# Gated linear attention and a two-layer feed-forward block in one kernel: the first weight matrix in its own row order, attention in half chunks of 64 tokens

## The chip, the cores and the metric

The kernel runs on one core of one Trainium2 chip. The metric is device time in microseconds for one execution of the whole program. The core has a matrix engine (TensorE, PE in the profile, with its weight loads as PEld), a vector engine (VectorE, DVE), a scalar engine (ScalarE, ACT), GpSimd (POOL), and SyncE (SP), which here issues every DMA transfer. Each engine takes its own instructions in order; engines wait for each other through semaphores. Matmul results go to PSUM, which the kernel splits into eight banks.

## The reference

Four batches, eight heads, 768 tokens, head size 48. The recurrence keeps a 48×48 state for each batch and head:

```python
for t in range(S):
    state = alpha[:, :, t, :, None] * state + einsum('bhd,bhe->bhde', k[:, :, t], v[:, :, t])
    y[:, :, t] = einsum('bhd,bhde->bhe', q[:, :, t], state)
x = y.transpose(0, 2, 1, 3).reshape(3072, 384)
h = x @ w_in                       # 384 x 2048, arrives as float64
g = h * clip(h + 3, 0, 6) / 6
out = g @ w_out                    # 2048 x 384, arrives as float64
```

## The kernel before

**Tiling.** Tokens are cut into 24 chunks of C = 128, six to a batch. Heads are handled in pairs (NP = 4): a pair fills 128 partitions, each head padded from 48 to 64. For a chunk the cumulated decay R and its inverse P come from two scans on VectorE (`decay`, `growth`); keys are multiplied by R and queries by P (`scaled`), so that within a chunk the recurrence is a masked matrix product, and across chunks a product with one state. Two chunks form a group of 256 tokens for the feed-forward part.

**Attention steps of a chunk.** `scores` forms keys × queries: below chunk 8 in eight full 128×128 products, from chunk 8 (SWAP) in halves, leaving out the quarter that the mask would erase. `masked` multiplies the result by the triangle into A on VectorE. `within` multiplies A by v in blocks of 32 output rows; from chunk 8 it needs a copy of half of v (`keep_v`, into v0, on ScalarE). `across` adds the product of the state with the queries, 12 matmuls of 128 columns, in every chunk but the first of a batch. `keep_x` copies the sum out of PSUM as x. For the state, keys are needed with tokens on partitions: below chunk 8 by transposes on TensorE (`k_by_token`, `keep_k`), from chunk 8 through memory outside the core (`turn_k` in 32×32 blocks on VectorE, `write_k` in one transfer, `read_k` in four). `update` multiplies them by v into a 128-partition block whose useful parts are two 48×48 corners a pair; `next_state` adds these to the decayed state on VectorE in two instructions of 48 partitions, and `decayed_state` multiplies by the next chunk's decay on GpSimd. The last chunk of a batch needs no update.

**Feed-forward.** Groups 0 and 1 use plain products (`ff1`, `ff2`). From group 2 the first layer is computed in 20 products of quarter size with sums before and after (M on TensorE, `combine_x` and `output1` on VectorE, `keep1` on ScalarE, the gate `gate1`/`hidden1` on ScalarE and VectorE), and from group 1 the second in 7 products (P on TensorE, `combine_g` and `output2` on VectorE). The float64 weights arrive as pairs of 32-bit words in 16 slices (`load_weight`) and are turned into float32 by bit operations on ScalarE, VectorE and GpSimd (steps d1, d2, dx, d3, d4).

**What sets the order.** One long list of words, written out by hand or by a tool, gives the order of all steps: a word such as `sc.9.1.2` is step, chunk and PSUM banks. Each engine gets its share of the list in that order. The first layer's rows are loaded in the order `(p t r)`, 32 partitions at a time, because `within` and `across` put pair p at partitions 32p of x:

```python
return ps_t["y", j][32 * p : 32 * p + 32, kk]        # L516, y_of
```

Four of the eight PSUM banks serve attention (`bank_t`), four the feed-forward part. The words `z` are matmuls on the identity that only keep TensorE busy at the start. Lines: scores L383, L385 (from chunk 8) and L408; masks L391 and L416; v copies L399; transposes to tokens L428; key turns L453 and L455; key write L459 and read L466; decay L471; update L488 and L494; state sums L507 and L509; within L529, L533 and L539; across L549; first layer L693, its copies L699; second layer L796; weight transfers L184 and L187.

Of the kernel before, what the change touches and what calls it, by code (L numbers as in the profile page):

```python
# [17 lines left out]
def kernel(  # L18
# [43 lines left out]
    GT = G * C  # L62
    W = C + 1
# [3 lines left out]
    HB = C // 2  # L67
# [10 lines left out]

    tri = consts.tile([C, 3, HB], mybir.dt.bfloat16, tag="tri")
    nc.gpsimd.memset(tri, 1.0)  # L80
    for n, b in ((0, 0), (0, 1), (2, 0), (1, 1)):
        at = slice(HB * b, HB * b + HB)
        nc.gpsimd.tensor_copy(out=tri[at, n], in_=mask[at, at])

    v0 = consts.tile([C, H, 64], FP, tag="vfirst", name="vfirst")
    nc.gpsimd.memset(v0, 0.0)
# [9 lines left out]
    for r in range(max(NR, NV)):  # L96
        for name, pad, n in (("a", 1.0, NR), ("k", 0.0, NR), ("q", 0.0, NR), ("v", 0.0, NV)):
            if r >= n:
                continue
            if name == "v":  # L100
                t = consts.tile([C, H, 64], FP, tag=f"v{r}", name=f"v{r}")
            else:
                t = rings[:, 3 * r + "akq".index(name)]
            eng = nc.vector if r == 0 else nc.gpsimd
            if name == "v":
                t4 = t.rearrange("s (p a) e -> s p a e", a=2)
                eng.memset(t4[:, :, 0, D:64], pad)
                eng.memset(t4[:, :, 1, 0 : 64 - D], pad)
            else:
                eng.memset(t[:, :, D:64], pad)  # L110
            ring[name, r] = t
# [16 lines left out]
    st, sm = [], []  # L128
    for r in range(2):
        t = consts.tile([C, NP, 2 * D], FP, tag=f"st{r}")  # L130
        nc.gpsimd.memset(t, 0.0)
        st.append(t)
    for r in range(2):
        t = consts.tile([C, NP, 2 * D], FP, tag=f"sm{r}")
        nc.gpsimd.memset(t, 0.0)
        sm.append(t)
# [35 lines left out]
    def load_weight(i):  # L172
        u = 2 if wide else 1
        dst = weight_dst(i)
        m = dst.shape[1]
        to = raw_of(i).rearrange("p (m n) w -> p m (n w)", m=m) if wide else dst
        if i < NW1:
            n = NSL // KT
            src = moe_w_in[:, u * i * n : u * (i + 1) * n].rearrange(
                "(p t r) f -> p r t f", p=NP, t=KT)  # L180

            for p in range(NP):
                queue = nc.sync
                queue.dma_start(out=to[32 * p : 32 * p + 32], in_=src[p])  # L184
        else:
            o = (i - NW1) * m * C
            nc.sync.dma_start(  # L187
                out=to, in_=moe_w_out[o : o + m * C, :].rearrange("(f p) n -> p f n", p=C))
# [45 lines left out]
    def add_low(i):  # L234
# [9 lines left out]
    bank_t = [ps.tile([C, NP, C], FP, tag=f"t{i}", name=f"t{i}_ps") for i in range(4)]  # L244
    Rs, Qs, Ks, kbs, As = (
        [consts.tile([C, *shape], FP, tag=f"{name}{r}", name=f"{name}{r}") for r in range(2)]
        for name, shape in (("R", (NP * W,)), ("q", (NP, C)), ("k", (NP, C)), ("kb", (NP, C)),
                            ("A", (H, C))))
    Ps = consts.tile([C, NP * W], FP, tag="P", name="P")

    def bank(name, j, i):
        ps_t[name, j] = bank_t[i]
        return ps_t[name, j]
# [35 lines left out]
    def load_v(j, z):  # L289
        v_t[j] = ring["v", z]  # L290
        to = v_t[j].rearrange("s (p a) e -> s p a e", a=2)
        sv = rows(v, j).rearrange("(p a) s d -> s p a d", a=2)
        if j >= SWAP:
            for b in range(2):
                for g in range(2):
                    at = slice(HB * (b ^ g), HB * (b ^ g) + HB)
                    for a in range(2):
                        e = (64 - D) * a
                        nc.sync.dma_start(
                            out=to[HB * b : HB * b + HB, 2 * g : 2 * g + 2, a, e : e + D],  # L300
                            in_=sv[at, 2 * g : 2 * g + 2, a])
            return
        nc.sync.dma_start(out=to[:, :, 0, 0:D], in_=sv[:, :, 0])
        nc.sync.dma_start(out=to[:, :, 1, 64 - D : 64], in_=sv[:, :, 1])
# [65 lines left out]
    SWAP = 8  # L370

    def score_blocks(t):
        return t.rearrange("s p r -> s (p r)")[:, 0 : 2 * 3 * HB].rearrange(
            "s (x n t) -> s x n t", x=2, n=3)

    def scores_of_halves(j, *at):
        sc = [bank("sc%d" % o, j, at[o]) for o in range(2)]
        for h in range(H):
            p, a = divmod(h, 2)
            r, g = slice(64 * a, 64 * a + D), p // 2  # L380
            to = score_blocks(sc[a])[:, p % 2]
            k, q = K_t[j][r, p], Q_t[j][r, p]
            nc.tensor.matmul(to[HB * g : HB * g + HB, 0 : 2 + g : 1 + g], k[:, 0:HB],  # L383
                             q.rearrange("r (n t) -> r n t", n=2), start=True, stop=True)
            nc.tensor.matmul(to[HB * (1 - g) : HB * (2 - g), 1 + g], k[:, HB:C], q[:, HB:C],  # L385
                             start=True, stop=True)

    def masked_halves(j):
        A_t[j] = As[j % 2]
        for o in range(2):  # L390
            nc.vector.tensor_tensor(  # L391
                out=score_blocks(A_t[j][:, NP * o : NP * (o + 1)]),
                in0=score_blocks(ps_t.pop(("sc%d" % o, j))),
                in1=tri.unsqueeze(1).to_broadcast([C, 2, 3, HB]), op=ALU.mult)

    def keep_v(j):
        for b in range(2):
            at, h = slice(HB * b, HB * b + HB), slice(NP * b, NP * b + NP)
            nc.scalar.copy(out=v0[at, h], in_=v_t[j][at, h])  # L399

    def scores(j, *at):
        if j >= SWAP:
            return scores_of_halves(j, *at)

        sc = [bank("sc%d" % o, j, at[o]) for o in range(2)]
        for h in range(H):
            r = slice(64 * (h % 2), 64 * (h % 2) + D)
            nc.tensor.matmul(sc[h % 2][:, h // 2], K_t[j][r, h // 2], Q_t[j][r, h // 2],  # L408
                             start=True, stop=True)

    def masked(j):
        if j >= SWAP:
            return masked_halves(j)
        A_t[j] = As[j % 2]
        for o in range(2):
            nc.vector.tensor_tensor(  # L416
                out=A_t[j][:, NP * o : NP * (o + 1)], in0=ps_t.pop(("sc%d" % o, j)),
                in1=mask.unsqueeze(1).to_broadcast([C, NP, C]), op=ALU.mult)
# [4 lines left out]
    def k_by_token(j, i=None):  # L423
        if not last(j):
            t = bank("kb", j, i)
            for p in range(NP):
                if j < SWAP or p < 2:
                    nc.tensor.transpose(t[:, p], K_t[j][:, p], ident)  # L428
                    continue
                for b in range(2):  # L430
                    nc.tensor.transpose(t[HB * b : HB * b + HB, p],
                                        K_t[j][:, p, HB * (1 - b) : HB * (2 - b)], ident)
# [579 lines left out]
```

## Time and profile before

| | |
|---|---|
| median of three runs | 547.78 us (547.0 to 548.17) |
| the profiled execution's own time | 547.54 us |
| its span, first to last instruction | 545.8 us |
| TensorE busy | 537.1 us, 98% of the span |
| VectorE busy | 476.9 us, 87% |
| ScalarE busy | 202.9 us, 37% |
| GpSimd busy | 51.9 us, 10% |
| DMA queue q1 | 98448 packets, 51.87 MB, 38.9% of 16 engines |

The page gives the busy time of each engine, the chain of work that ended last (followed back from the last instruction to whatever released each step), groups of instructions by line, and the transfers. In the lists of groups a line reads: line, engine, operation, output and inputs with shapes, count, then busy time and mean duration, then the engine's idle time ahead of them. Durations of consecutive instructions overlap, so the distance between two starts is the cost in a full stretch.

### The profile page before, as it was taken

To read this page: it belongs to the slowest core of one execution; us is meant where nothing else is said; L and a number is where in the kernel's file an instruction comes from. 1 tells how busy PE (TensorE), PEld (TensorE's weight loads), DVE (VectorE), ACT (ScalarE), POOL (GpSimd) and SP (SyncE) were. 2 spreads that over 40 slices of the span, in tenths; PEclk is the share of its full clock that TensorE was granted. 3 is DMA by queue.
4 is the path that set the end of the run, shared out by engine and by line. 5 is a ranking of instruction groups with operands and counts; after the bars stand their busy time and mean duration, and the time that the engine had idled before them with its cause. 6 is when DMAs were issued, how large, how long until landed. Compare 5 with 4: busy or idle time off the path is not lost.

```text
span 545.8 us, 14868 instructions
## 1 busy us (share of the span) xinstructions
PE 537.1 (98%) x6222; PEld 511.3 (94%) x6222; DVE 476.9 (87%) x822; ACT 202.9 (37%) x358; POOL 51.9 (10%) x76
## 2 busy tenths in 40 slices
PE   8999999999999999999999999999999999999997
PEld 8888977789899999999999999999999999999996
DVE  7989989999999999999999999999899796465471
ACT  2666664003443342353233233333334332342330
POOL 3333334200000000000000000000000200000000
PEclk9999999999999999999999999999999999999999
DMA  9996677140433552343535342335353110000001
GB/s 182 210 222 127 203 228 186 41 121 17 89 88 81 151 154 49 85 121 89 136 83 154 98 100 49 84 89 157 73 132 95 44 23 16 8 3 23 23 0 37
DMA packets 98515, 52.82 MB, mean 97 GB/s; under 512 B 51472, under 2 KB 91664, under 8 KB 98448
## 3 DMA queue, kind: packets, MB, share of 16 engines
q1 hardware_dynamic: 98448, 51.87, 38.9%
q8 instruction: 49, 0.80, 0.6%
q14 instruction: 18, 0.15, 0.1%
HBM read 43.71 MB, written 8.13 MB: 95 GB/s over the span
## 4 chain that ended last, share of the span: by engine, by line
PE 78%; DVE 12%; DMA 5%; SPq 3%; issue 1%; ACT 0%; POOL 0%; DVEq 0%; POOLq 0%
PE m_ps L796 32%; PE m_ps L693 30%; PE m_ps L571 3%; DMA raw<-in_moe_w_in_dram 2%; PE t_ps L549 2%; PE t_ps L383 2%; PE t_ps L529 1%; PE m_ps L625 1%; SPq L284 1%; PE t_ps L533 1%; DMA g_sb<-in_moe_w_in_dram 1%; DVE g_sb L740 1%; PE t_ps L314 1%; DVE rings L740 1%; PE t_ps L488 1%
## 5 line engine op out<-in xcount | busy, mean ns | idle before, releaser
L699 ACT COPY g_sb<-m_ps 128x512 f32<-128x512 f32 x110 | 63.8, 585 | 158.9 <-PE m_ps L693 130.5
L796 PE MATMUL m_ps<-w,g_sb 128*128 128x192 f32 x704 | 121.7, 326 | 0.0
L796 PEld LDWEIGHTS m_ps<-w,g_sb 128*128 128x128 f32 x704 | 113.8, 190 | 0.6 <-issue 0.2
L796 PE MATMUL m_ps<-rings,g_sb 128*128 128x192 f32 x528 | 91.3, 326 | 0.7 <-DVE rings L740 0.7
L796 PEld LDWEIGHTS m_ps<-rings,g_sb 128*128 128x128 f32 x528 | 85.3, 190 | 1.3 <-issue 1.3
L693 PE MATMUL m_ps<-xc,w 128*128 128x128 f32 x640 | 83.9, 277 | 0.1
L693 PEld LDWEIGHTS m_ps<-xc,w 128*128 128x128 f32 x640 | 77.9, 192 | 2.4 <-issue 1.0
L587 ACT ACTIVATE r<-g_sb,half 128x512 f32<-128x512 f32 x80 | 56.7, 722 | 56.3 <-DVE g_sb L630 18.4
L591 DVE SCALAR_TENSOR_TENSOR g_sb<-r,g_sb 128x512 f32<-128x512 f32 x80 | 53.8, 691 | 7.4 <-ACT r L587 7.3
L693 PE MATMUL m_ps<-xT,raw 128*128 128x128 f32 x400 | 51.8, 276 | 0.0
L471 POOL TENSOR_TENSOR t<-t,R 128x384 f32<-128x384 f32 x20 | 18.5, 926 | 331.7 <-DVE t L509 202.9
L693 PEld LDWEIGHTS m_ps<-xT,raw 128*128 128x128 f32 x400 | 48.5, 192 | 0.4
L740 DVE TENSOR_TENSOR g_sb<-g_sb 128x512 f32<-128x512 f32 (+1 forms) x55 | 44.2, 835 | 0.7 <-PE m_ps L796 0.5
L693 PE MATMUL m_ps<-xT,w 128*128 128x128 f32 x320 | 41.5, 276 | 0.0
L693 PEld LDWEIGHTS m_ps<-xT,w 128*128 128x128 f32 x320 | 39.1, 192 | 0.2
L341 DVE TENSOR_TENSOR_SCAN R<-t,ones 128x516 f32<-128x516 f32 x24 | 31.0, 1292 | 4.0 <-ACT t L332 2.9
L630 DVE TENSOR_TENSOR g_sb<-g_sb 128x512 f32<-128x512 f32 x40 | 27.1, 689 | 7.4 <-ACT g_sb L699 7.4
L571 PE MATMUL m_ps<-xT,w 128*128 128x256 f32 x144 | 32.2, 380 | 1.0 <-POOL w L238 1.0
L693 PE MATMUL m_ps<-xc,raw 128*128 128x128 f32 x240 | 32.2, 277 | 0.0
L571 PEld LDWEIGHTS m_ps<-xT,w 128*128 128x128 f32 x144 | 27.0, 190 | 5.1 <-POOL w L238 1.4
L352 DVE TENSOR_TENSOR_SCAN P<-t 128x516 f32<-128x516 f32 x24 | 30.7, 1279 | 0.2
L693 PEld LDWEIGHTS m_ps<-xc,raw 128*128 128x128 f32 x240 | 29.7, 192 | 0.7 <-issue 0.4
(121 smaller groups left out, 734.8 us busy)
## 6 DMA issues: line engine op xcount, KB each, us to landing
raw<-in_moe_w_out_dram SPq DMA_DIRECT2D x8, 768.0 KB, 5.0
raw<-in_moe_w_in_dram SPq DMA_DIRECT2D x24, 192.0 KB, 6.2
out_dram<-oh SPq DMA_DIRECT2D x44, 96.0 KB, 1.8
kq<-in_k_dram SPq DMA_DIRECT2D x36, 96.0 KB, 2.4
aq<-in_alpha_dram SPq DMA_DIRECT2D x36, 96.0 KB, 2.4
qq<-in_q_dram SPq DMA_DIRECT2D x36, 96.0 KB, 2.5
far<-kq SPq DMA_DIRECT2D x13, 256.0 KB, 2.4
kb<-far SPq DMA_DIRECT2D x52, 64.0 KB, 2.0
```

Source lines behind the costliest of these rows:

```text
L341: nc.vector.tensor_tensor_scan(out=reverse(R, n - 1, n), data0=reverse(ax, n, n), data1=reverse(ones, n, n), initial=0.0, op0=ALU.mult, op ...
L352: nc.vector.tensor_tensor_scan(out=P_t[j], data0=aX[j % 2][:, 0:n], data1=ini[j % 2], initial=0.0, op0=ALU.mult, op1=ALU.add)
L383: nc.tensor.matmul(to[HB * g : HB * g + HB, 0 : 2 + g : 1 + g], k[:, 0:HB], q.rearrange("r (n t) -> r n t", n=2), start=True, stop=True)
L471: nc.gpsimd.tensor_tensor(out=st[j % 2], in0=sm[j % 2], in1=R_t[j][:, :, 0:1].to_broadcast([C, NP, 2 * D]), op=ALU.mult)
L571: nc.tensor.matmul(h[:, f], w1[:, kk, o : o + C], xT_t[g][:, kk], start=(kk == 0), stop=(kk == KT - 1))
L587: nc.scalar.activation(out=to, in_=h, func=AF.Relu, bias=half, scale=1.0 / 6.0)
L591: nc.vector.scalar_tensor_tensor(out=to, in0=r, scalar=1.0, in1=h, op0=ALU.min, op1=ALU.mult)
L630: eng.tensor_tensor(out=out, in0=in0, in1=in1, op=ALU.add if s1 > 0 else ALU.subtract)
L693: nc.tensor.matmul(acc[g][i][:, f * C : (f + 1) * C], spots[w][:, f * C : (f + 1) * C], x_of(g, x), start=(first and f == 0), stop=last, s ...
L699: nc.scalar.copy(out=slots[z], in_=acc[g][i])
L740: nc.vector.tensor_tensor(out=out, in0=in0, in1=in1, op=ALU.subtract)
L796: nc.tensor.matmul(to[g], a, rhs[:, f], start=(first and f == 0), stop=(last and f == HF - 1), skip_group_check=True)
```

## The change

The first weight matrix is loaded in its own row order, 128 partitions in one transfer a slice instead of four of 32, and `y_of` now places 32-row block number 3p + kk of x accordingly. Attention treats every chunk as two halves of 64 tokens. A and v become tiles with one block for each half. In the block of half b, the 64 rows of that half hold masked scores (in A) and v (in v); the other 64 rows hold the queries (in A) and the state (in v). One matmul over all 128 rows then gives within and across together (`attend`, steps ya and yb). `place_q` and `place_state` (qa, sv) are the copies on ScalarE that fill these rows; for the first half of a batch GpSimd writes zeros instead. Scores are 16 matmuls of 64×64 for all chunks, in two banks. Updates are 16 matmuls of 64×64 in two banks, one for each half, and the state becomes a tile of 48 columns a pair, on all partitions: `next_state` is now one addition after each half (step sm, twice). The last chunk of a batch updates its first half. The key trip writes in four transfers with pieces of 32 values and reads in one. The list of words is new throughout. The separate steps vh (`keep_v`), yi (`within`) and yx (`across`) are gone. Numbers of words, before and after: kb and ck 7 and 8, kt, kw and kr 13 and 16, u 20 and 24, sm 20 and 44, qa and sv 0 and 48 each, vh 16 and 0, yi 24 and 0, yx 20 and 0, ya and yb 0 and 24 each.

Lines that are new or stay; the removed ones stand above:

```diff
     ring = {}
     rings = consts.tile([C, 3 * NR, H, 64], FP, tag="rings")
+    for r in range(NR):
+        for name, pad in (("a", 1.0), ("k", 0.0), ("q", 0.0)):
+            t = ring[name, r] = rings[:, 3 * r + "akq".index(name)]
+            (nc.vector if r == 0 else nc.gpsimd).memset(t[:, :, D:64], pad)
+
+    vs, As = [], []
+    for r in range(NV):
+        t = consts.tile([C, 2, H, 64], FP, tag=f"v{r}", name=f"v{r}")
+        nc.gpsimd.memset(t, 0.0)
+        vs.append(t)
+    for r in range(2):
+        t = consts.tile([C, 2, H, HB], FP, tag=f"A{r}", name=f"A{r}")
+        nc.gpsimd.memset(t, 0.0)
+        As.append(t)
...
         if i < NW1:
             n = NSL // KT
+            nc.sync.dma_start(out=to, in_=moe_w_in[:, u * i * n : u * (i + 1) * n].rearrange(
+                "(t p) f -> p t f", p=C))
         else:
             o = (i - NW1) * m * C
...
     def load_v(j, z):
+        v_t[j] = vs[z]
+        to = v_t[j].rearrange("s b (p a) e -> s b p a e", a=2)
         sv = rows(v, j).rearrange("(p a) s d -> s p a d", a=2)
+        for b in range(2):
+            at = slice(HB * b, HB * b + HB)
+            for a in range(2):
+                e = (64 - D) * a
+                nc.sync.dma_start(out=to[at, b, :, a, e : e + D], in_=sv[at, :, a])
     def transposed(name, j, i=None):
         if j >= FIRST:
...
+    def scores(j, *at):
+        sc = ps_t["sc", j] = [banks[i][:, 0 : NP * HB].rearrange("s (p t) -> s p t", p=NP)
+                              for i in at]
+        for p in range(NP):
+            for b in range(2):
+                half = slice(HB * b, HB * b + HB)
+                for a in range(2):
+                    r = slice(64 * a, 64 * a + D)
+                    nc.tensor.matmul(sc[a][half, p], K_t[j][r, p, half], Q_t[j][r, p, half],
+                                     start=True, stop=True)
+
+    def masked(j):
         A_t[j] = As[j % 2]
+        sc = ps_t.pop(("sc", j))
         for b in range(2):
+            half = slice(HB * b, HB * b + HB)
+            to = A_t[j][half, b].rearrange("s (p a) t -> s a p t", a=2)
+            for a in range(2):
+                nc.vector.tensor_tensor(
+                    out=to[:, a], in0=sc[a][half],
+                    in1=mask[half, half].unsqueeze(1).to_broadcast([HB, NP, HB]), op=ALU.mult)
+
+    def place_q(j, b):
+        if (j % NC, b) == (0, 0):
+            return
+        at, half = HB * (1 - b), slice(HB * b, HB * b + HB)
+        to = As[j % 2][at : at + D, b].rearrange("d (p a) t -> d a p t", a=2)
+        for a in range(2):
+            nc.scalar.copy(out=to[:, a], in_=Q_t[j][64 * a : 64 * a + D, :, half])
     def last(j):
         return j % NC == NC - 1
     def k_by_token(j, i=None):
+        t = bank("kb", j, i)
+        for p in range(NP):
+            nc.tensor.transpose(t[:, p], K_t[j][:, p], ident)
     def keep_k(j):
+        kb_t[j] = kbs[j % 2]
+        nc.scalar.copy(out=kb_t[j], in_=ps_t.pop(("kb", j)))
...
         to = k_in_blocks(j).rearrange("r (v p c) -> r p v c", v=V, p=NP)
         src = K_t[j].rearrange("r p (v s) -> r p v s", v=V)
+        nc.vector.transpose(out=to, in_=src)
     def write_k(j):
+        far_t[j] = far.tile([BLK, V, NP, V, BLK], FP, tag="far", name="far")
+        for o in range(V):
+            nc.sync.dma_start(out=far_t[j][:, :, :, o].rearrange("s v p c -> s (v p) c"),
+                              in_=k_in_blocks(j)[BLK * o : BLK * (o + 1)].rearrange(
+                                  "s (w c) -> s w c", c=BLK))
     def read_k(j):
         kb_t[j] = kbs[j % 2]
+        nc.sync.dma_start(out=kb_t[j].rearrange("s p r -> s (p r)"),
+                          in_=far_t.pop(j).rearrange("s v p o c -> v s (p o c)"))
     def decayed_state(j):
         if j % NC:
+            nc.gpsimd.tensor_tensor(out=st, in0=sm, in1=R_t[j][:, :, 0:1].to_broadcast([C, NP, D]),
+                                    op=ALU.mult)
+
+    def place_state(j, b):
+        at = HB * (1 - b)
+        if (j % NC, b) == (0, 0):
+            nc.gpsimd.memset(v_t[j][at : at + HB, b], 0.0)
             return
+        to = v_t[j][at : at + D, b].rearrange("d (p a) e -> d a p e", a=2)
+        for a in range(2):
+            e = (64 - D) * a
+            nc.scalar.copy(out=to[:, a, :, e : e + D],
+                           in_=(half_st if b else st)[64 * a : 64 * a + D])
+
+    def update(j, *at):
+        for b, i in enumerate(at):
+            ps_t["u", j, b] = banks[i][:, 0 : NP * D].rearrange("r (p n) -> r p n", p=NP)
         for p in range(NP):
             for a in range(2):
+                for b in range(len(at)):
+                    half, e = slice(HB * b, HB * b + HB), (64 - D) * a
+                    nc.tensor.matmul(ps_t["u", j, b][64 * a : 64 * a + 64, p],
+                                     kb_t[j][half, p, 64 * a : 64 * a + 64],
+                                     v_t[j][half, b, 2 * p + a, e : e + D],
+                                     start=True, stop=True)
+
+    def next_state(j, b):
+        u = ps_t.pop(("u", j, b))
+        if (j % NC, b) == (0, 0):
+            nc.vector.tensor_copy(out=half_st, in_=u)
+        else:
+            nc.vector.tensor_tensor(out=(half_st, sm)[b], in0=u, in1=(st, half_st)[b], op=ALU.add)
     def y_of(j, kk, p):
+        t, n = divmod(KT * p + kk, 4)
+        return ps_t["y", j][32 * n : 32 * n + 32, t]
+
+    def attend(j, b, i=None):
+        if b == 0:
+            bank("y", j, i)
         for n in range(4 * NP):
             i, p = divmod(n, NP)
             a, e = divmod(i, 2)
+            nc.tensor.matmul(y_of(j, (i + 1) // 2, p)[:, HB * b : HB * b + HB],
+                             v_t[j][:, b, 2 * p + a, 32 * e : 32 * e + 32],
+                             A_t[j][:, b, 2 * p + a], start=(b == 0 and i == 0), stop=(i != 1),
                              skip_group_check=True)
     xTs = [consts.tile([C, KT, GT], FP, tag=f"xT{r}", name=f"xT{r}") for r in range(2)]
```

The start of the new list, which orders everything anew (in the old one the first weight slice, w.0, is the thirteenth load):

```diff
+        run("""z.0.2 z.0.3 z.0.8 z.0.3 z.0.1 qa.0.0 la.0 ta.0.0 ca.0 la.1 ta.1.0 ca.1 lk.0 r.0
+               tk.0.1 k.0 p.0 r.1 kb.0.2 ck.0 w.0 d2.0 d3.0 lq.0 z.0.5 tq.0.3 q.0 p.1 z.0.3 d1.0
+               dx.0 d4.0 qa.0.1 la.2 lv.0.0 u.0.0.1 sm.0.0 sv.0.1 sc.0.2.3 m.0 ta.2.0 ca.2 r.2 w.2
...
```

## The prediction

> **What bounds the kernel now.** I read three views in this order: the chain that ended last, the busy time by stretches, and single blocks in order of time. The chain, by engine:
>
> ```profile
> PE 78%; DVE 12%; DMA 5%; SPq 3%; issue 1%; ACT 0%; POOL 0%; DVEq 0%; POOLq 0%
> ```
>
> The stretches (length, then busy time and instruction count of PE, PEld, DVE, ACT, POOL, then clock, DMA share, GB/s):
>
> ```profile
> 0.00:42.00 42.00, 39.45 (x522) 35.87 (x523) 35.27 (x59) 22.59 (x29) 15.68 (x35) 1.00 1.02 206
> 42.00:98.00 56.00, 55.01 (x356) 44.98 (x355) 52.84 (x72) 31.37 (x41) 20.42 (x20) 1.00 0.67 177
> 98.00:140.00 42.00, 41.13 (x352) 36.32 (x351) 41.57 (x65) 7.84 (x16) 3.17 (x8) 1.00 0.30 73
> 140.00:410.00 270.00, 269.70 (x3592) 263.77 (x3592) 261.20 (x475) 96.69 (x189) 9.70 (x11) 1.00 0.41 102
> 410.00:482.00 72.00, 72.00 (x982) 70.86 (x981) 52.16 (x93) 26.72 (x52) 2.92 (x3) 1.00 0.12 34
> 482.00:546.00 64.00, 59.83 (x426) 59.52 (x424) 33.89 (x63) 17.71 (x34) 0.00 (x0) 0.99 0.06 18
> ```
>
> To see: TensorE sets the end, but VectorE is nearly as full. From 98 to 410 us it idles 9.2 of 312 us. Its slack lies after 410 us (50 of 136 us), when attention runs dry. The first 42 us are full on DMA.
>
> What attention costs, TensorE in order of time (start, us, instructions; distances between starts are what counts, an fp32 matmul is two passes):
>
> ```profile
> 140.90 1.16 PE L408 MATMUL t_ps<-q,k 48*128 48x128 f32 x16
> 141.99 1.16 PE L693 MATMUL m_ps<-xT,w 128*128 128x128 f32 x8
> ...
> 167.24 0.32 PE L383 MATMUL t_ps<-q,k 48*64 48x128 f32 x1
> ...
> 168.09 1.16 PE L693 MATMUL m_ps<-xc,w 128*128 128x128 f32 x8
> ...
> 187.46 0.65 PE L529 MATMUL t_ps<-A,vfirst 128*32 128x64 f32 x32
> 187.93 0.63 PE L533 MATMUL t_ps<-A,v 128*32 128x64 f32 x32
> 188.37 0.84 PE L549 MATMUL t_ps<-q,t 128*32 128x128 f32 x24
> 189.14 1.16 PE L693 MATMUL m_ps<-xc,w 128*128 128x128 f32 x8
> ```
>
> Scores take 1.09 us a chunk below chunk 8 and 0.85 after; "within" 0.47+0.44; "across" 0.66 (0.77 less 0.11 of switching); the updates of two chunks 0.81 (202.54 to 203.35), 0.41 each, 0.50 below chunk 8. And VectorE groups:
>
> ```profile
> L391 DVE TENSOR_TENSOR A<-t_ps,tri 128x384 f32<-128x384 f32 x32 | 16.2, 548 | 0.2
> L416 DVE TENSOR_TENSOR A<-t_ps,mask 128x512 f32<-128x512 f32 x16 | 10.3, 682 | 1.1 <-PE t_ps L408 1.0
> L509 DVE TENSOR_TENSOR t<-t_ps,t 48x192 f32<-48x192 f32 x32 | 11.2, 349 | 1.0 <-PE t_ps L488 0.7
> ```
>
> **What the Trainium skill says.** TensorEngine Tiling, "64×64 Mode": four independent tiles; this trace has them in the halved scores. TensorE: Matmul & The Clock Gate, "LDWEIGHTS": a load costs by its columns, about P/1.2 ns; here 64 columns take 133 ns and 32 take 110, 0.72 ns a column, so it agrees roughly. DMA: Bandwidth & Descriptors, "Specifications": pieces under 512 B lose line rate; the new key write has 128 B pieces, which no row here shows. Same page, section on the semaphore of 16: the engines used must divide the slowest dimension of both sides; the new single read has 4 there, an estimate of 4 engines instead of 16, also not shown.
>
> **TensorE, by part.** *Across* goes: 20×0.65 = −13.0. *Scores* become 16 matmuls of 64 columns in four quadrants. Today a quadrant has 8 passes of 96 columns on average in 0.85 us: 106 ns each, against 82 of streaming (192 columns take 163 ns: 2.60 us for 16), so 25 over. With 64 columns: 8×(54+25) = 0.63. Bounds 0.47 (as L529) and 0.85. Saved 16×0.22+8×0.46 = −7.2. *Updates* in quadrants: 8×(41+25) = 0.53, +1.8 for the 20 there are; bounds 0.41 and 0.65. Four new ones, one for each batch's last chunk, half as many: +1.6, and four transposes for chunk 5, +0.45. *Attend* twice 0.46 replaces "within": 0. Runs of tiled blocks between full-array work go from 37 to 39, 0.21 us each: +0.4. Sum −16.0: were TensorE alone to decide, the span would be 529.8.
>
> **VectorE, by part.** Spacing between starts is less than a duration: pairs of L391 take 0.93, of L416 1.20 us. That makes 1.04 ns an element plus 0.07. *Masks* are now four of 64 partitions × 256: 0.33 each if they overlap as those do. But L509's pairs, on 48 partitions, do not overlap (0.355 each for 0.349); without it a mask is 0.43. I take 0.38: 1.52 a chunk, +0.32 or +0.59. *State*: two additions of 192 columns on all 128 partitions, 0.27 (as L812 spaces) to 0.355; 44 instead of 40. *Key turn*: one 512-wide transpose at 0.955 (L318's spacing) for 0.75 in three (431+2×268 ns less overlaps); 16 instead of 13: +5.5. All: 477 to about 494 us.
>
> **ScalarE, GpSimd, SP.** The 32 copies of v go (12.9 us). 88 copies place q (256 wide, 403 ns by that row: 35 us) and 88 the state (192 wide, about 350: 31 us): 203 to 257 us of some 540. Cover: 159 us in which L699 waits for TensorE. Without cover two state copies, 0.7 us, stand before each attend half. GpSimd's decay halves (20×926 ns); its start-up fills grow by about 1.3 us (five of 1024 columns at twice 524 ns, for 3.9 removed), beside the first loads; four 64-row fills of a few tenths follow, one a batch. SP: w_in 32 issues to 8, v 144 to 96, key trips 65 to 80. *The weight slice in one transfer*: same bytes, same 2 KB runs, and the queues are already full (1.02, 206 GB/s), so I book 0; bounds −3 (768 KB of w_out land in 5.0 us, quarter slices in 6.2 to 7.5) and +2. *Key trip*: one write of 2.4 and four reads at 0.49 an issue and 2.0 to landing, some 6.7 us; now four writes and a read, 6 to 11. On SP the read stands behind the landed write and holds the next loads; VectorE's turns wait for those. The new order leaves 11 to 24 us of TensorE work between turn and update (before, 10 to 34), so hidden: 0, up to +5. *Order*: the first slice is now the fourth load instead of the thirteenth and chunks 2 and 3 come later; TensorE starts with 17 of its 29 fillers; DMA paces both orders here, booked 0.
>
> **The sum on the path.** In the old order the masks of chunks 20 and 21 are done at 409.6 us, VectorE having idled 19.0 until then. TensorE needs them only later: chunk 21's output is copied at 436.0, so there is 26 us of cushion. Then 46 products of the first layer (M), 22 of the second (P) and two chunks' attention remain, 109.8 us. In the new order, from chunk 21's attend, exactly 46 M and 22 P remain too, and four attends (1.9 more), two half updates (0.8), less two "across" and cheaper scores (1.7): 110.9 us. And VectorE's list before that mask grew: masks +6.6 (22 chunks at 0.33), state +1.8, key turns +4.4, and feed-forward and scan steps moved ahead of it (h +5, s +6, o +3, p, xc, G: +11.8). Together +24.6. The middle values for masks and state add 2.6. Of the idle I take 7 back, since 8.6 of the 19.0 fell between 139 and 410 us, where TensorE was the slower: 409.6+24.6+2.6−7 = 429.8. The cushion is gone; TensorE waits at attends. 429.8+110.9 = 540.7. What is late next is nothing: the rest is TensorE's. Around the span lie 1.7 us (547.54 − 545.8), and the profiled run is 0.2 under the median 547.78: 542.6, said as **543.0**.
>
> **Rivals.** *The full TensorE gain*: 529.8+1.7 = 531.5. For it: every attention block shrinks on an engine that carries 78% of the chain. Against: VectorE would have to reach chunk 21's mask 11 us earlier than summed, idling nearly nothing. *Slower, VectorE waits*: VectorE works in order, and each chunk now sends it through update, first half sum, second half sum, decay on GpSimd, placement on ScalarE. If it stands 0.5 us a chunk at a half sum or at a copy held behind L699's waits, 22 chunks give +11: 554. It decides from 6 us over the forecast, 0.28 us a chunk (from 548.9). For it: ScalarE's placements sit behind copies that waited 130 us for TensorE. Against: today L509 waits 1.0 us in 32. *The one transfer does nothing*: no rival of the time, as it is booked at 0.
>
> **How the numbers follow.** Measurement tells 0.2% (1.1 us) from nothing. VectorE-bound middle 48%: own range 537 to 549, of it faster 40, same 5, slower 3. Full gain 22%, all faster. Waits 30%: slower 29, same 1. So faster 0.62, same 0.06, slower 0.32. Range 532 to 553: below it two fifths of the full-gain case, above it a third of the last, together under 2 in 10.
>
> **What would show it.** After: L549's kind gone, scores near 0.63 us and updates near 0.53 a chunk; mask instructions near 415 ns, spaced 0.33 or 0.43; VectorE busy near 494; TensorE with gaps before attends and scores up to chunk 21, whose mask ends near 430 us, then about 111 us. No such gaps and VectorE at 410 to 420 there: full gain. Long VectorE waits at half sums: the slower rival. I am wrong altogether if the first 60 us differ by more than 5 us, or updates wait for key reads.

## The result, and the profile after

The changed kernel takes 550.25 us (median of 20, 547.65 to 553.24), the kernel before 547.75 (median of 20): the ratio is 1.0045, with a 95% interval of 1.003 to 1.0061. It is a little slower, by 2.5 us, where 543.0 and "faster" were forecast. Its times scatter more than those of the kernel before (546.87 to 548.88), and the profiled execution, at 553.01 us with a span of 551.2, lies 2.8 us above their median, so the losses read from its trace are on the high side. All times here are of fast executions; the only slow one, 588.77 us in a later experiment at a clock of 0.875, is left out.

The chain that ended last, by engine, now reads:

```profile
PE 82%; DVE 10%; DMA 5%; issue 1%; SPq 1%; ACT 0%; POOL 0%; DVEq 0%; POOLq 0%
```

The stretches (length, then busy time and instruction count of PE, PEld, DVE, ACT, POOL, then clock, DMA share, GB/s):

```profile
0.00:42.00 42.00, 31.33 (x441) 28.49 (x442) 34.42 (x57) 25.56 (x37) 17.74 (x27) 0.88 0.90 221
42.00:98.00 56.00, 55.68 (x662) 47.29 (x661) 53.38 (x80) 41.48 (x70) 19.16 (x24) 1.00 0.79 191
98.00:140.00 42.00, 42.00 (x359) 36.22 (x358) 41.60 (x71) 10.22 (x24) 3.21 (x6) 1.00 0.22 48
140.00:410.00 270.00, 263.58 (x3414) 257.81 (x3414) 251.07 (x460) 125.23 (x262) 7.67 (x13) 0.99 0.43 96
410.00:482.00 72.00, 72.00 (x820) 71.05 (x819) 62.95 (x114) 33.14 (x71) 1.55 (x3) 1.00 0.33 75
482.00:546.00 64.00, 64.00 (x616) 63.49 (x615) 38.94 (x72) 21.07 (x40) 0.00 (x0) 1.00 0.04 12
```

Two stretches differ most. In the first 42 us TensorE works 31.3 us instead of 39.5, and the clock that it was granted is 0.88 of full speed instead of 1.00. Between 140 and 410 us it stands still 6.4 us instead of 0.3, and VectorE is *less* busy there than before (251.1 for 261.2): the forecast had VectorE as the bound of just this stretch.

The second loss stands in the list by time (start, us, then the instruction; in brackets the idle time and what ended it). SP's own issues around chunk 12's keys, then TensorE:

```profile
229.79 2.64 SPq L399 DMA_DIRECT2D far<-kq  x4
232.52 3.71 SPq L275 DMA_DIRECT2D v<-in_v_dram  x4
236.28 2.02 SPq L262 DMA_DIRECT2D qq<-in_q_dram  x4
238.40 0.85 SPq L726 DMA_DIRECT2D out_dram<-oh  x2
239.30 0.58 SPq L405 DMA_DIRECT2D kb<-far  x1
...
242.29 1.06 PE L602 MATMUL m_ps<-xc,w 128*128 128x128 f32 x8
246.61 1.10 PE L431 MATMUL t_ps<-v,kb 64*64 64x48 f32 x32 [3.26 <-DMA kb<-far]
247.50 1.10 PE L349 MATMUL t_ps<-q,k 48*64 48x64 f32 x32
```

The read of the keys is issued 9.5 us after their write, behind values, queries and two stores, and then needs 7.3 us. TensorE stands still 3.3 us for it, and what follows is slow: the granted clock is 0.52 from 246 to 252 us, and the 32 score passes take 1.10 us here, against 0.66 below. Over the 16 chunks whose keys go this way, the read is issued 4.8 to 13.1 us after the first write. Undisturbed, the new blocks look like this:

```profile
308.12 0.68 PE L431 MATMUL t_ps<-v,kb 64*64 64x48 f32 x32
308.62 0.66 PE L349 MATMUL t_ps<-q,k 48*64 48x64 f32 x32
309.21 1.05 PE L602 MATMUL m_ps<-xT,w 128*128 128x128 f32 x7
```

From start to start an update costs 0.50 us and the scores 0.59. The new groups on VectorE and ScalarE (count, busy us, mean ns, idle time before them):

```profile
L359 DVE TENSOR_TENSOR A<-t_ps,mask 64x256 f32<-64x256 f32 x96 | 36.0, 413 | 0.6
L394 DVE STREAM_TRANSPOSE kq<-k 128x512 f32<-128x512 f32 x16 | 11.3, 704 | 0.1
L441 DVE TENSOR_TENSOR s<-t_ps,st 128x192 f32<-128x192 f32 x20 | 6.9, 347 | 5.2 <-PE t_ps L431 5.0
L369 ACT COPY A<-q 48x256 f32<-48x256 f32 x88 | 35.5, 403 | 2.5 <-DVE q L335 1.4
L421 ACT COPY v<-s 48x192 f32<-48x192 f32 x48 | 16.8, 351 | 15.1 <-DVE s L441 13.3 <-DVE s L439 1.1
```

**Where TensorE's time went.** I added up the distances between the starts of all matmuls. What a distance has above 0.12 us, when it is longer than 0.45 us, counts as standing still; the rest belongs to the step. "Four reads" is the first experiment below.

| us | before | after | four reads |
|---|---|---|---|
| attention, updates and key transposes | 71.5 | 56.9 | 56.3 |
| standing still, to 42 us | 1.4 | 10.3 | 11.1 |
| standing still, 42 to 110 us | 1.2 | 0.4 | 0.4 |
| standing still, from 110 us | 1.6 | 7.1 | 0.4 |
| all else (feed-forward, fillers, ends) | 470.1 | 476.5 | 472.2 |
| span | 545.8 | 551.2 | 540.4 |

So the change does save TensorE 14.6 us. Standing still takes back 13.6 of it, in two places, and the rest of TensorE's work, the same instructions as before, takes 6.4 us longer, among it the idle matmuls at the start (2.1 more) and the half matmuls of the first layer (1.3). With four reads 2.1 of these 6.4 us remain; some 2.4 of the difference lie in idle matmuls and transposes of the start, which that edit leaves as they are, and so belong to the one profiled execution.

### The profile page after: what moved, and what is told of

Its sections match the earlier page's. It is cut to its first block, busy times and chain, and to the rows that moved or that the text cites. A ratio compares the mean times of both kernels' runs of the same rounds, so it can differ in the third digit from the quotient of the medians.

```text
span 551.2 us, 15132 instructions
## 1 busy us (share of the span) xinstructions
PE 530.0 (96%) x6306; PEld 505.5 (92%) x6306; DVE 482.4 (88%) x849; ACT 257.0 (47%) x503; POOL 49.3 (9%) x71
## 4 chain that ended last, share of the span: by engine, by line
PE 82%; DVE 10%; DMA 5%; issue 1%; SPq 1%; ACT 0%; POOL 0%; DVEq 0%; POOLq 0%
PE m_ps L705 33%; PE m_ps L602 28%; PE m_ps L480 5%; PE t_ps L456 4%; DMA kb<-far 4%; PE m_ps L518 3%; PE t_ps L431 2%; PE t_ps L349 2%; PE m_ps L491 2%; PE m_ps L534 2%; DVE R L312 1%; PE t_ps L285 1%; DVE A L359 1%; DVE P L323 1%; DVE q L335 1%
## 5 line engine op out<-in xcount | busy, mean ns | idle before, releaser
L705 PE MATMUL m_ps<-w,g_sb 128*128 128x192 f32 x704 | 123.0, 329 | 0.0
L705 PEld LDWEIGHTS m_ps<-w,g_sb 128*128 128x128 f32 x704 | 115.2, 192 | 0.5
L602 PE MATMUL m_ps<-xc,w 128*128 128x128 f32 x640 | 82.7, 277 | 0.2 <-DVE g_sb L543 0.2
L602 PE MATMUL m_ps<-xT,raw 128*128 128x128 f32 x400 | 53.0, 280 | 0.0
L410 POOL TENSOR_TENSOR st<-sm,R 128x192 f32<-128x192 f32 x20 | 12.3, 613 | 363.7 <-DVE sm L441 234.3
L649 DVE TENSOR_TENSOR g_sb<-g_sb 128x512 f32<-128x512 f32 (+1 forms) x55 | 41.8, 790 | 2.7 <-PE m_ps L705 2.2
L602 PEld LDWEIGHTS m_ps<-xT,w 128*128 128x128 f32 x320 | 39.4, 192 | 0.1
L369 ACT COPY A<-q 48x256 f32<-48x256 f32 x88 | 35.5, 403 | 2.5 <-DVE q L335 1.4
L359 DVE TENSOR_TENSOR A<-t_ps,mask 64x256 f32<-64x256 f32 x96 | 36.0, 413 | 0.6
```

What stands on the lines that cost most here:

```text
L359: nc.vector.tensor_tensor(out=to[:, a], in0=sc[a][half], in1=mask[half, half].unsqueeze(1).to_broadcast([HB, NP, HB]), op=ALU.mult)
L369: nc.scalar.copy(out=to[:, a], in_=Q_t[j][64 * a : 64 * a + D, :, half])
L602: nc.tensor.matmul(acc[g][i][:, f * C : (f + 1) * C], spots[w][:, f * C : (f + 1) * C], x_of(g, x), start=(first and f == 0), stop=last, s ...
L649: nc.vector.tensor_tensor(out=out, in0=in0, in1=in1, op=ALU.subtract)
L705: nc.tensor.matmul(to[g], a, rhs[:, f], start=(first and f == 0), stop=(last and f == HF - 1), skip_group_check=True)
```

## The experiments

All ratios are to the kernel before, run beside each experiment. Where two versions are compared, the difference is that of their ratios times 547.7 us, unless the text says otherwise; the medians differ from it by up to 1.3 us. "Four reads" always means the first experiment.

### The keys' way back

**Four reads instead of one.**

```diff
-        nc.sync.dma_start(out=kb_t[j].rearrange("s p r -> s (p r)"),
-                          in_=far_t.pop(j).rearrange("s v p o c -> v s (p o c)"))
+        to = kb_t[j].rearrange("s p r -> s (p r)")
+        src = far_t.pop(j).rearrange("s v p o c -> v s (p o c)")
+        for n in range(V):
+            nc.sync.dma_start(out=to[BLK * n : BLK * (n + 1)], in_=src[n])
```

> The changed kernel, but each chunk's keys are read back in four transfers of 32 partitions instead of one of 128. Theory A (late keys): in the changed kernel's trace the one read lands 6.4 to 7.3 us after its issue and TensorE stands still up to 3.3 us at the state update, with a lower clock afterwards, in all about 8 to 11 us between 240 and 320 us. Then the read lands in 2 to 4 us, the waits of the update on the read vanish and the time falls from 550 to 540 to 543 us. Rival C (VectorE sets the end, as forecast): the waits only change their name and the time stays at 548 to 551. Theory B (the start is what costs): also 548 to 551, since the start is untouched.

Measured: 542.72 us, ratio 0.9922 (0.9904 to 0.994). That is 6.7 us less than the changed kernel (7.5 by the medians), and now faster than the kernel before. The stretches of four reads:

```profile
0.00:42.00 42.00, 30.69 (x454) 27.62 (x455) 35.71 (x59) 26.81 (x39) 17.85 (x27) 0.92 0.94 224
140.00:410.00 270.00, 269.49 (x3544) 263.96 (x3543) 259.34 (x476) 129.57 (x271) 7.65 (x13) 1.00 0.43 98
482.00:546.00 64.00, 54.58 (x387) 54.28 (x386) 31.72 (x54) 16.50 (x32) 0.00 (x0) 0.99 0.05 15
```

The middle is full again; the first 42 us are no better than they were. What the profile says of the keys' tile, first in the changed kernel, then with four reads:

```profile
L405 SPq DMA_DIRECT2D kb<-far x16: 558/574/632, 157.4 to 476.7; - x16
  DMA kb<-far: 7.9, 5
```

```profile
L408 SPq DMA_DIRECT2D kb<-far x64: 319/419/1532, 155.8 to 467.1; - x64
DMA to landing us min/median/max: 1.9/2.0/3.5
```

The 7.9 us of standing in front of the one read (matmuls and their weight loads, some 4 us each) are gone, for four issues of 0.42 us instead of one of 0.57. So are the other 3 us or so of standing still from 110 us on, which the trace puts down to other causes. Reading earlier in the list, or writing in one piece again, was not tried.

**Two reads of 64 partitions** (the same loop over two).

> The changed kernel with the keys read in two transfers of 64 partitions. By its packets the single read has 3 to 4 in flight at a time and lands 6.4 to 7.3 us after its issue; the four have 5 to 8 and land after 2.0. If the number of transfers in one read sets how many engines carry it, two land after 3 to 4.5 us, and the time lies near that of four, 542 to 546. If it is the size of the row alone, two land like one and the time stays at 549 to 551.

Measured: 578.71 us, ratio 1.055 (1.0512 to 1.0587): not between one and four but 28 us worse than one. The keys' tile:

```profile
L408 SPq DMA_DIRECT2D kb<-far x32: 516/542/1349, 156.5 to 503.5; - x32
  DMA kb<-far: 24.2, 14
```

The packets of 2 KB tell why. They take about 100 ns each in all three kernels (102 to 110 in the mean), but at any moment (median) 4 are under way with one read, 2 with two, and about 7 with four (2 to 9 by chunk). The last packet ends some 5.4, 8.1 and 3.0 us after the first issue, and with two reads TensorE stands still 22.7 us from 110 us on, for 7.1 with one. The Trainium skill, DMA: Bandwidth & Descriptors, section "Why a DMA increments its semaphore by 16 and not by 1", says that a transfer goes to the largest number of engines up to 16 that divides the slowest dimension of both sides, and on this path to the lowest-numbered ones. One read has 4 there, and each of two has 2, which by the page is the same two engines for both; a read of 32 partitions has 32 and can use 16. The packet counts agree with the first two; about 7 for the third says only that it isn't held to 4. Which engines carried the packets does not stand in the trace.

### What bounds the rest

**VectorE lighter: masks of the second half left out from chunk 8**, on four reads (`if b and j >= FAR: continue` ahead of the mask).

> The changed kernel with the keys in four reads, and the two masks of the second half left out from chunk 8 on (the scores of that half are then not taken over, so this part of the attention is not computed). This takes 32 operations of 0.375 us, 12 us, off VectorE and nothing off TensorE. Rival C, the forecast's bound (VectorE's work up to the mask of chunk 21 sets the end): 530 to 536 us. If TensorE has been full since 60 us, as its busy row says, 541.5 to 543.5, no change.

Measured: 542.43 us, ratio 0.9898 (0.988 to 0.9915), which overlaps that of four reads; the span is 540.7 us for 540.4. Its middle and end:

```profile
140.00:410.00 270.00, 269.72 (x3545) 264.24 (x3544) 249.96 (x452) 130.05 (x272) 9.42 (x13) 1.00 0.44 98
482.00:546.00 64.00, 54.95 (x391) 54.66 (x389) 31.73 (x54) 16.88 (x32) 0.00 (x0) 1.00 0.05 15
```

VectorE has 9.4 us less to do in the middle, and the end comes no earlier. VectorE's total does not set it.

**TensorE lighter: the second attend left out from chunk 8**, on four reads (`if b and j >= FAR: break` in its loop).

> The changed kernel with the keys in four reads and without the attention matmuls of the second 64 tokens from chunk 8 on (that half of the attention output is not computed). It takes 16 times 64 matmuls off TensorE, about 0.5 us each time, 8 us, and nothing off VectorE. If TensorE sets the end from 60 us on, the time falls by 6 to 8.5 us, to 534 to 537. If VectorE, ScalarE or a transfer does, by less than 2 us, 541 to 543.

Measured: 536.49 us, ratio 0.9799 (0.9784 to 0.9814), 6.7 us below four reads (6.2 by the medians) for about 7.5 us of work:

```profile
482.00:546.00 64.00, 49.03 (x345) 48.73 (x343) 26.56 (x46) 13.32 (x27) 0.00 (x0) 0.99 0.05 14
```

Four reads has only 0.4 us of standing still from 110 us on, so it is the work and not a wait that was taken away: TensorE sets the end. Together the two decide, for the kernel with four reads, against the forecast's bound.

**The first weight matrix alone, on the kernel before** (one transfer a slice, `y_of` placed to match).

> The kernel before with only the first weight matrix in natural row order, one transfer a slice instead of four, and the attention output's 32-row blocks placed to match. If this part is worth nothing, as booked, 547 to 548.5 us (before: 547.8). If slower landing slices are what starves the start of the changed kernel, 550 us or more; if the three issues saved each time count, 545 or less.

Measured: 548.44 us, ratio 1.0015 (1.0007 to 1.0023). This part costs at most 1.3 us and explains none of the start: TensorE stands still 1.4 us to 42 us, as before.

### The start

TensorE waits in the first 66 us of four reads mainly for VectorE:

```profile
PE t_ps L458 <- DVE q L335: 2.8, 1, 2.8
PE t_ps L285 <- DVE s L443: 1.7, 1, 1.7
...
PE t_ps L377 <- DVE k L335: 0.9, 1, 0.9
...
PE t_ps L349 <- DVE q L335: 0.9, 1, 0.9
```

By 36 us VectorE has worked about as much as in the kernel before (29.9 us for 30.7), but on other things: 8.0 instead of 4.7 us on decoding weights, and the masks of two chunks instead of four.

**The start of the kernel before, chunks 0 to 3, without and with four reads** (the words up to chunk 3's output in the old order, then the rest of the new list).

> The changed kernel with the order of the kernel before for chunks 0 to 3 and the weight slices 0, 1, 3 and 4; from there on its own order. Theory B (the new order starves TensorE in the first 40 us): TensorE's work is back at 39 to 40 us busy in the first 42 us, and the time falls by 8 to 13 us, to 537 to 542. Rival: the decoding that is put off only starves TensorE at the weights of slices 5 to 11 instead, so that the gain is given back by 100 us and the time is 548 to 551. Theory A alone: 549 to 551, since the late keys lie after 140 us.

> The two edits together: four reads for the keys, and the start of the kernel before. If both theories hold and are separate losses, the gains add up: 527 to 533 us, with TensorE busy 97 to 99 per cent of the span. If VectorE bounds the middle at what was forecast, the end cannot come before 540 to 544, whichever of the two helped alone.

Measured: 575.42 us, ratio 1.0519 (1.0482 to 1.0555), and 569.1, 1.0397 (1.0372 to 1.0422). Both expectations fell, but not cleanly. SP's waits in the first 66 us of the former:

```profile
SPq L162 <- POOL w L217: 26.5, 2, 22.7
```

A weight load stood 22.7 us in SP's queue behind a slot that GpSimd had still to empty, and from 42 to 60 us the transfers stood nearly still (DMA share 0.01). This tests the joint of two lists more than it tests the start.

**The old order up to the last weight slice**, on four reads, values loaded later than there.

> The changed kernel with the keys in four reads, and the order of the kernel before up to the last decoded weight slice (chunks 0 to 5, all slices), with chunk 0's loads before chunk 1's, the values loaded after the gates and keys, and the new steps set beside those that they serve; from there on the changed kernel's own order. Unlike the earlier attempt with chunks 0 to 3 the slices keep the order in which the kernel before loads them. Theory B (order alone makes the start slow): chunk 5's output is copied with TensorE 6 to 11 us behind its own work instead of 20.6, and the time falls from 542.7 to 529 to 535 us. Rival (the halves themselves make the start slow: the state sum, its copy and the second attend stand in line in each chunk, with nothing else for TensorE to do): 541 to 550 us.

Measured: 576.62 us, ratio 1.0526 (1.0508 to 1.0543). TensorE's two longest waits are again for loads and what stands behind them:

```profile
PE t_ps L377 <- DVE k L335: 10.9, 1, 10.9
PE t_ps L433 <- DMA v<-in_v_dram: 9.3, 1, 9.3
```

**The same with those loads moved up.**

> As the changed kernel with four reads and the order of the kernel before up to the last slice, with the values of chunk 5, the keys and the queries of chunk 6 loaded ahead of the last two weight slices, since TensorE stood still 9.3 us for those values and 10.9 us for keys behind them. Those 20 us and the low clock after them should go: 548 to 556. Theory B in its first form (order alone makes the start slow) would still say 529 to 535; the rival, that the halves make each of the chunks 1 to 3 take about 10 us instead of 6 in this order too, says above 545.

Measured: 563.79 us, ratio 1.0294 (1.0279 to 1.0309). Better by 13 us, still far off: in this list TensorE stands still 13.6 us from 110 us on. But its start can be read: the outputs of chunks 0 to 3 are copied at 21.1, 29.4, 38.3 and 50.6 us, where the kernel before has 18.0, 22.5, 30.6 and 36.9. With attention first, too, the new form is slower there.

**And without the copies of queries and states in chunks 0 to 5.**

> The kernel with four reads and the order of the kernel before up to the last slice, second form (563.8 us), without the copies that set queries and states beside the weights and values in chunks 0 to 5 (those chunks lack what comes from earlier tokens). In its trace with them the outputs of chunks 1, 2 and 3 follow at 8.3, 8.9 and 12.3 us, against 4.5, 8.1 and 6.3 in the kernel before. If the line state sum, copy, second attend is what makes chunks slow when attention goes first, chunk 3's output comes at 38 to 43 us instead of 50.6. If the loads, VectorE or the transposes of the keys do it, at 47 us or later.

Measured: 557.99 us, ratio 1.0174 (1.0143 to 1.0206), chunk 3's output at 46.0 us, between the two answers. The line of sum, copy and second attend, together with ScalarE's time for the copies, is worth 4.6 of the 13.7 us by which that order is late; the rest is something else.

**Without those copies, in the new order with four reads.**

> The changed kernel with the keys in four reads, without the copies that set queries and states beside the weights and values in chunks 0 to 5 (so those chunks lack what comes from earlier tokens). It takes about 18 us of copies off ScalarE in the first 110 us, and with them the line from the state sum through the copy to the second attend. If these copies and their line are what holds the start back, the gap of TensorE to its own work at chunk 5 (20.6 us) falls to 8 to 14 and the time to 530 to 537. If the weights' decoding on VectorE holds it back whatever the attention does, 540 to 543.

Measured: 542.35 us, ratio 0.9902 (0.9886 to 0.9919), no difference from four reads that can be told. In the new order these copies on ScalarE are not what the start waits for.

**Queries copied by GpSimd in chunks 0 to 5.**

> The changed kernel with the keys in four reads, and in chunks 0 to 5 the queries are copied by GpSimd instead of ScalarE: 22 copies of 0.41 us, 9 us off an engine that is busy 16 of 18 us between 42 and 60 us. If ScalarE's load is what is late in the start, 537 to 541; if not, or if GpSimd delays the last step of the decoding instead, 542 to 546.

Measured: 544.79 us, ratio 0.9955 (0.9939 to 0.9972), 1.8 us worse.

**One stretch of the new order rearranged**, on four reads:

```diff
-d2.1 d3.1 u.1.0.1 sm.1.0 ca.3 r.3 lq.2 tq.2.2 q.2 lk.2 tk.2.3 k.2 lq.3 tq.3.0 dx.1 d4.1 sm.1.1 p.3 qa.1.1 sv.1.1
+u.1.0.1 lq.2 tq.2.2 sm.1.0 q.2 sm.1.1 ca.3 lk.2 tk.2.3 k.2 d2.1 qa.1.1 sv.1.1 d3.1 r.3 lq.3 tq.3.0 dx.1 d4.1 p.3
```

> The changed kernel with the keys in four reads (542.7 us), and one stretch of its order between chunks 1 and 2 rearranged: the sums of chunk 1's states and the scaling of chunk 2's queries and keys come ahead of the decoding of slice 1 and of chunk 3's decay scan on VectorE. In the kernel with four reads TensorE stands still 1.7 us for the state sum and 2.8 us for the scaled queries there, and works at about half clock for 6 us after it. Theory B (what is left beside TensorE's own work is lost in this start): both waits go and the time falls by 4 to 7 us, to 536 to 539. Rival C (VectorE's total bounds the end): its work is only moved, so 542 to 544.

Measured: 541.98 us, ratio 0.9885 (0.987 to 0.99), 2.0 us better by the ratios and 0.7 by the medians; the span in its profile, 540.5, is that of four reads. Chunk 1's output comes 3.2 us earlier, chunk 2's at 63.0 us for 63.3: TensorE stands 2.0 us less before 42 us and 2.4 us more after, and its longest stop, 2.8 us, is now for GpSimd's last step of slice 1. By its median it is the fastest version here that computes everything, 6 us below the kernel before.

**Idle matmuls in the remaining stop of that version** (22 ahead of the half matmuls of slice 1).

> The changed kernel with four reads and the rearranged stretch (541.98 us), with 22 idle matmuls ahead of the first half matmuls of slice 1, where TensorE stands still 3 us and then works 4 to 6 us at a lower clock. They fill the 3 us and cost nothing if the wait outlasts them. If the low clock is part of the start's loss: the clock stays at 1.00 from 28 to 40 us and the time falls by 1 to 2.5 us, to 539.5 to 541. If the work after it waits for VectorE anyway, 541.5 to 543.

Measured: 542.43 us, ratio 0.9903 (0.9888 to 0.9918). The profile's mean clock is 1.00 for 0.995, and the time is the same: the low clock is not what costs there.

**Decoding made lighter, late and early**, both on four reads: the masking of the shifted bits left out in eleven slices, and VectorE's whole part left out in slices 0 to 3 (`if i < 4: return` in `high_bits`).

> The changed kernel with four reads, and without the masking of the shifted bits in the decoding of the eleven slices that are not decoded by halves (their weights are then wrong): 11 operations of about 0.6 us on VectorE, 7 us, all before 105 us, and nothing less on TensorE. If VectorE sets the pace of the start, the time falls by 4 to 7 us, to 535.5 to 538.5. If the transfers of weights, ScalarE or GpSimd do, by less than 2 us: 541 to 543.

> The changed kernel with four reads and without VectorE's part in the decoding of the first four slices (0 to 3; their weights are then wrong): 9 operations, 8.0 us by the trace, which its order puts ahead of the attention of chunks 1 to 3 before 36 us. TensorE stands still 11.1 us before 42 us there. If this decoding ahead of attention is what keeps TensorE waiting, that falls to 3 to 6 us and the time by 5 to 9 us, to 534 to 538. If the line of half sums or the loads keep it waiting, 541 to 543 with 9 us or more of standing still.

Measured: 541.29 us, ratio 0.9894 (0.9878 to 0.9911), and 539.74, 0.9862 (0.9845 to 0.988). The first takes 7 us from VectorE, one operation of it before 36 us, and gains 1.5, which its interval does not separate from four reads. The second takes 8.0 us before 36 us and gains 3.3, less than expected; its first stretch:

```profile
0.00:42.00 42.00, 34.09 (x490) 30.32 (x490) 29.76 (x53) 29.08 (x42) 16.59 (x27) 1.00 0.94 224
```

TensorE stands still 7.5 us there instead of 11.1, now for a decay's transfer (1.5), the copy of a decay on ScalarE (1.1) and scaled keys (0.9), among others. So the decoding that the new order puts ahead of attention costs about a third of the start's loss. Take it away and other things, nearly as late, take its place: from 20 to 40 us the transfers' share is then 0.99, ScalarE works 16.4 of the 20 us and VectorE 14.7.

## Why the prediction was wrong, and where it was right

**TensorE's sum: right.** −16.0 us was worked out, −14.6 and, undisturbed, −15.2 were measured. Scores take 0.59 us for 0.63 and updates 0.50 for 0.53; attend in place of "within" and "across" saves 12.5 for 13.0. The four new half updates were booked at 1.6 us where the prediction's own 0.53, halved and taken four times, gives 1.1; all updates together cost 4.4 us more than before, for 3.4 booked. The weight loads that the prediction reads from the trace, 133 and 110 ns, agree with the P/1.2 beside them (53 and 27 ns) in their difference, not in size; no term rests on that. From the PE-only span of 529.8 one comes to the 551.2 of the changed kernel by 1.4 less saved, 13.6 more standing still and 6.4 of slower work, and to the 540.4 of four reads by 0.8, 7.7 and 2.1.

**"So hidden: 0, up to +5": the first step that failed.** The key trip was put at 6 to 11 us with 11 to 24 us of cover. Chunk 12's takes 16.8 us from the write's first issue to the first matmul of the update that waits for it: 9.5 us until SP comes to the read, since the read stands behind loads and stores that the list puts between, and 7.3 us for the read. For the second part the prediction had named the cause, a slowest dimension of 4 on four engines, and gave it no price of its own; the first part it did not have, since it put the read behind the landed write but not behind the loads and stores between. Undoing this one transfer gives 6.7 us back, more than the upper bound of 5.

**"DMA paces both orders here, booked 0": the second step that failed.** In the first 42 us TensorE stands still 10.3 us instead of 1.4. DMA is about as full as before (0.90 and 221 GB/s for 1.02 and 206), so its share could not tell what TensorE would find to do. About a third is decoding ahead of attention. The cause of the rest stays open: I could not build an order for the new form that starts as fast as the kernel before, and no single load taken off an engine brings the rest back. That an order exists which does is neither shown nor excluded.

**"VectorE-bound middle": the third, the bound.** "Of the idle I take 7 back" expected 12 us of VectorE idling until chunk 21's mask, and that mask at 429.8 us. It idled 31.3 us in the changed kernel, mask at 438.9, and 21.0 us with four reads, mask at 428.0. The last is close to the forecast and means nothing: with 12 us of masks left out the end does not move. I had read a nearly full VectorE as the next bound because its sum grew; it follows TensorE. That four reads, with 542.72 us, comes out at the forecast of 543.0 is luck: the forecast's 11 us above the PE-only span are of the right size, but they come mostly from the start and not from VectorE. The rival of the full TensorE gain had the bound right: from 110 us on four reads stands still 0.4 us. What kept it from its 531.5 is mostly the start.

**VectorE's sizes.** A mask costs 36.0/96 = 0.375 us (0.38 taken), a state sum 0.35 (the upper bound). The key turn was mis-sized: 0.704 us instead of 0.955, 4 us in 16. VectorE's busy time is 482.4 instead of 494; the other 7.6 us I did not take apart.

**ScalarE and the weight transfer: right.** 257.0 us busy for 257 worked out. The one transfer costs 0.8 us, within its bounds of −3 and +2.

**The slower rival** named waits at half sums and copies. The idle time in front of L441 does rise, to 5.2 us, but what it waits for is the update, which waits for the keys; and leaving out the copies in chunks 0 to 5 makes no difference. The measured 550.25 lies where this rival decides, from 548.9 up, but through other causes. The two signs that the prediction set against itself, a first 60 us that differs by more than 5 us and updates that wait for key reads, are the two that came.

## What to carry to other kernels

What a transfer costs can hang on the shape that it is issued in, as the key read did here: look at the slowest dimension of both sides, count the packets under way, and price the landing from that, before booking it as hidden behind a lead; and count the lead from the issue that the queue's order really gives. A busy share near that of the bound does not make an engine the next bound: take work off it and see whether the end moves. A start in which the transfers are nearly full and several engines work most of the time shouldn't be booked at nothing when its order is rewritten.

## What the runs showed of the hardware

Splitting a read in two made it slower than one, and splitting it in four made it faster: 2, 4 and about 7 packets under way, 8.1, 5.4 and 3.0 us to the last packet's end. A 512-wide block transpose on VectorE takes 704 ns in the key turn, and 1.12 us in the turn of loaded chunks (L289, same size); the patterns differ, and I did not test which part of them decides. The key write's pieces of 128 bytes take about 12 ns each in the packets of the trace, 2048 of them in some 3.3 us (2.6 to 3.9 by chunk).
